# A decode layer: K and V in 4 MB transfers, weights ahead of K, and the output halves in two column tiles

## The chip, the cores and the metric

The kernel runs on one core of a Trainium2 chip. The metric is the device time of one launch in microseconds (us). The time before the change is 224.56 us, the median of three runs (223.5, 224.56, 224.62).

## What is computed

One decode step for four sequences (B = 4), one new position each, width D = 576. Two branches start from the same x and are added to it.

```python
def _A_ref(x, k_cache, v_cache, wq, wo):        # attention; 32 query heads, 16 K/V heads, Dh = 128
    W = 2048                                    # only the last 2048 of 8192 cached positions
    q = (x @ wq).reshape(B, 1, 32, 128)
    k, v = k_cache[:, :, Sk - W:], v_cache[:, :, Sk - W:]     # each serves two query heads
    p = softmax(q k^T * Dh ** -0.5)
    return (p v).reshape(B, 1, 4096) @ wo
def _B_ref(x, w1, w2, w3, w4):
    h = gelu(layernorm(x) @ w1)
    hs = shifted(h) @ w2                        # four groups of columns moved by 1 or 2 positions
    x1 = x + hs
    return x1 + gelu(layernorm(x1) @ w3) @ w4
xn = layernorm(x)
return x + _A_ref(xn, k_cache, v_cache, wq, wo) + _B_ref(xn, w1, w2, w3, w4)
```

With a single position the shifts move everything out, so `hs` is zero; the kernel multiplies w2 by a tile of zeros (`hs_inT`). All data are bfloat16. 88.5 MB come in: K and V 33.5 MB each, w3 and w4 5.3 MB each, wq and wo 4.7 MB each, w1 and w2 0.7 MB each. The output is 4 x 576.

## The kernel before, in words

**Order of work.** There is no scheduler. Every piece of work is entered by `add` (or `add_dma` for transfers) with an engine, the events that it waits for, the event that it signals, and a key; each engine's list is then sorted by key and written out. All large transfers are issued by SyncE (SP), in one queue, in the order of their keys (L171). Before it issues a transfer, SP waits for the events in its list, and everything behind it in the list waits too.

**Memory.** K and V pass through a ring of ten slots of 2 MB. A slot is 128 partitions of 16 KB: four heads of one sequence, 32 partitions to a head, 64 consecutive positions to a partition (`NU = 4`, `NT = 64`), so 16 chunks of K and 16 of V. Weights borrow slots that are free for a time: wq stands in slots 8 and 9 at the start, wo in slots 4 to 7 after K, w3 and w4 in slots that V has left.

**K stage.** A chunk's 64 blocks of 128 x 128 are transposed by TensorE against a permutation matrix, eight to a PSUM buffer (`pe_T`, L333; three buffers, `NTB`). VectorE and ScalarE copy them out (`evac`, L340 and L339). `pe_SC` (L351) multiplies them by the queries: four matmuls with 512 columns each, one for each head, go to the four 32-column tiles of the array. All 16 chunks add into four PSUM banks, with zeros in the padded queries `Qpad` for the rows of other heads.

**Softmax.** One reduction over the four banks gives the row maximum (L372), ScalarE takes the exponential bank by bank (L376), VectorE multiplies each bank by the head masks (L384, 16 instructions), and two rounds of matmuls (L393, L404), with copies by ScalarE (L402, L406), turn the probabilities so that positions lie on partitions.

**V stage.** For each chunk VectorE spreads the probabilities over the heads (`dve_pad`, L422), and `pe_PV` (L433) does 64 matmuls with V blocks as weights. V0 to V7 wait until K chunks 6 to 13 are transposed; V8 to V15 wait for PV0 to PV7. Between V7 and V8 the queue has w1, w2 and wo, which wait for the last probability turn (`PTy3`).

**MLP and end.** The small products (w1 at L493/L495, w2 at L503/L504), a layernorm (`ln_ops`) and x1's transpose (L283/L286) are placed among PV8 to PV12. wo is applied in three parts (`pe_AO`, L456) after PV7, PV11 and PV15; each needs a scaled copy (L472), selecting matmuls (L449) and a copy (L475). The product with w3 (`pe_h2`, L525 and L529, 180 matmuls) stands after the last wo part, then one gelu (L535), then w4 in five pieces of 18, 10, 5, 2 and 1 rows to a partition, each with its own transfer and its matmuls (also L456). wo and w4 add into the same two PSUM accumulators, one for each half of the 576 output columns: for each row of weights there is a 288-column matmul for the left half, then one for the right half, both with a 128 x 4 weight in the same array columns. VectorE and ScalarE copy one half each to SBUF (L550, L551), and SP and ScalarE store them.

The lines that the prediction's steps touch are L171 (all transfers), L333, L351, L372, L376, L384, L393, L422, L433, L456, L525/L529 and L550/L551.

Of the kernel before, what the change touches and what calls it, by code (L numbers as in the profile page):

```python
# [5 lines left out]
FP32 = mybir.dt.float32  # L6
# [6 lines left out]
NSLOT = 10  # L13
NKT = 12
NTB = 3
SC_LAG = 2
ACT_EVAC = (1, 4, 7)
N_WARM = 6
AO_CH = ((0, 4), (4, 6), (6, 8))
# [14 lines left out]
def bass_parallel_sum__sliding_block_cached__mixer_s_mlp__decode_kernel(  # L34
# [8 lines left out]
    NU = 4  # L43
# [11 lines left out]
    CH = [(b, gq) for gq in range(4) for b in range(B)]  # L55
# [3 lines left out]
    with ExitStack() as ctx:  # L59
# [5 lines left out]

        ring_t = sb("ring", [128, NSLOT * UE], BF16)
        regB_t = sb("regB", [128, NKT * 1024], BF16)
        PT_t = sb("PT", [128, NT * 32], BF16)
# [3 lines left out]
        ktgrp = regB_t[:].rearrange("p (s t u i) -> p s t u i", s=NKT // 2, t=16, u=NU)  # L72
        P4 = regB_t[:, 0:4 * NU * 512].rearrange("p (q t u i) -> p q t u i", q=4, t=16, u=NU)
        PTx = regB_t[:, 4 * NU * 512:4 * NU * 512 + 4 * 512].rearrange("p (q x) -> p q x", q=4)
        PTpad = regB_t[:, 0:2 * NT * 2 * NU].rearrange("p (s t u e) -> p s t u e", s=2, t=NT, u=NU)
        PTv = PT_t[:].rearrange("p (t c e) -> p t c e", t=NT, c=NC)

        wqmain = ring_t[:, 8 * UE:10 * UE].rearrange("p (r n) -> p r n", r=4)
        wqrag = PT_t[:, 0:Hq * Dh // 2]
        wo_a = ring_t[:, 4 * UE:4 * UE + 7 * 4 * D].rearrange("p (h r n) -> p h r n", h=7, r=4)  # L80
        _o = 2 * NT * 2 * NU
        wo_b = regB_t[:, _o:_o + 4 * D].rearrange("p (r n) -> p r n", r=4)
        _o += 4 * D
        w1main = regB_t[:, _o:_o + 4 * D].rearrange("p (r n) -> p r n", r=4)
        _o += 4 * D
        w1rag = regB_t[:, _o:_o + HALF]
        _o += HALF
        w2main = regB_t[:, _o:_o + 4 * D].rearrange("p (r n) -> p r n", r=4)
        _o += 4 * D
        w2rag = regB_t[:, _o:_o + HALF]  # L90
        _o += HALF
        assert _o <= NKT * 1024
        wo_at = lambda hg: wo_a[:, hg] if hg < 7 else wo_b
        w3r = [ring_t[:, 6 * UE + r * F:6 * UE + (r + 1) * F] for r in range(3)] + [ring_t[:, 8 * UE:8 * UE + F]]
        w3rag = ring_t[:, 6 * UE + 3 * F:6 * UE + 3 * F + FH]
        assert 3 * F + FH <= 2 * UE
# [23 lines left out]
        mask4 = sb("mask4", [128, NU], FP32)  # L120
        sel_f = sb("sel_f", [128, 32], FP32)
        sel_bf = sb("sel_bf", [128, 32], BF16)
# [3 lines left out]
        zeros_bf = sb("zeros_bf", [128, 512], BF16)  # L126
        rmax = sb("rmax", [128, 1], FP32)
# [7 lines left out]
        ORT = sb("ORT", [128, 4, 8, B], BF16)  # L135
        t1 = sb("t1", [B, D], FP32)
        out_sb = x1n_bf
# [4 lines left out]
        PTps = [ps[:, 4 + k, :].rearrange("p (t x) -> p t x", t=16) for k in range(4)]  # L142
        ACC = [ps[0:B, k, 0:HALF] for k in range(2)]
        ORps = ps[:, 2, 0:128].rearrange("p (r h b) -> p r h b", r=4, h=8)
        rinvps = ps[:, 3, 0:128]
        OTps = [ps[:, 6 - max(gq - 1, 0), 0:128] for gq in range(4)]
        QTps = ps[:, 7, 0:128]
        HSps = ps[0:B, 7, 128:128 + HALF]
        HTps = ps[:, 7, 416:440].rearrange("p (c b) -> p c b", b=B)
        XTps = [ps[:, 7, 440 + 12 * k:452 + 12 * k].bitcast(BF16).rearrange("p (c b) -> p c b", b=B) for k in range(3)]  # L150
        H2Tps = ps[:, 7, 0:144].rearrange("p (c b) -> p c b", b=B)
# [25 lines left out]

        KS = float(NB + 4)
# [6 lines left out]
        def pool_ident(t, tag, pattern, view, key):  # L185
# [11 lines left out]
        P(lambda e: e.memset(ones_f[:], 1.0), sig="ones_f", key=-89)  # L197


        add("dve", lambda e: e.tensor_reduce(out=mask4[:], in_=ident_f[:].rearrange("p (u x) -> p u x", u=NU), axis=AX.X, op=ALU.add),  # L200
            waits=["ident_f"], sig="mask4", key=-8)
        add("dve", lambda e: e.tensor_reduce(out=sel_f[:], in_=ident_f[:].rearrange("p (u x) -> p x u", u=NU), axis=AX.X, op=ALU.add),
            waits=["ident_f"], sig="sel_f", key=-8)
        add("dve", lambda e: e.tensor_copy(out=sel_bf[:], in_=sel_f[:]), waits=["sel_f"], sig="sel_bf", key=-7.9)
        add("dve", lambda e: e.tensor_reduce(out=mU[:], in_=ident_f[:].rearrange("p (i u) -> p u i", u=NU), axis=AX.X, op=ALU.add),
            waits=["ident_f"], sig="mU", key=-8)
        for x in range(2):
            add("dve", lambda e, x=x: e.tensor_copy(out=mU_bf[:, :, x], in_=mU[:]), waits=["mU"], sig=f"mU_bf{x}", key=-7.8)
# [3 lines left out]
        ev_wq = [add_dma([(ring_t[:, 8 * UE:10 * UE], A_wq[0:512, :].rearrange("(p r) n -> p (r n)", r=4))], "wq", (), -20),  # L212
                 add_dma([(wqrag, rag_src(A_wq))], "wqr", (), -15)]

        def kv_src(cache, c):
            b, gq = CH[c]
            return cache[b, NU * gq:NU * gq + NU, Sk - W:Sk, :].rearrange("g (i t) d -> i g (t d)", t=NT)

        k_slot = lambda c: c % NSLOT
        v_slot = lambda c: (6, 7, 8, 9, 0, 1, 2, 3)[c % 8]  # L220
        t_done = lambda c: f"T{NBLK * c + NBLK - 1}"
        ev_k, ev_v = [], []
        for c in range(NC):
            w = ["q"] if c in (8, 9) else ([t_done(c - NSLOT)] if c >= NSLOT else [])
            ev_k.append(add_dma([(slot(k_slot(c)), kv_src(A_k_cache, c))], ("ring", k_slot(c)), w, c))
        for c in range(NC):
            w = [f"PV{c - 8}"] if c >= 8 else [t_done(c + 6)]
            ev_v.append(add_dma([(slot(v_slot(c)), kv_src(A_v_cache, c))], ("ring", v_slot(c)), w, KS + c))
            if c == 7:
                free = ["PTy3"]  # L230
                ev_w1 = add_dma([(w1main, B_w1[0:512, :].rearrange("(p r) n -> p r n", r=4)), (w1rag, rag_src(B_w1))], "w1",
                                free, KS + c + 0.1)
                ev_w2 = add_dma([(w2main, B_w2[0:512, :].rearrange("(p r) n -> p r n", r=4)), (w2rag, rag_src(B_w2))], "w2",
                                free, KS + c + 0.2)
                wo_s = A_wo.rearrange("(h p r) n -> p h (r n)", h=8, r=4)
                ev_wo = add_dma([(wo_a.rearrange("p h r n -> p h (r n)"), wo_s[:, 0:7, :]),
                                 (wo_b.rearrange("p r n -> p (r n)"), wo_s[:, 7, :])],
                                "wo", [t_done(NC - 1)] + free, KS + c + 0.3)
        w3_src = B_w3[0:512, :].rearrange("(p r) n -> p r n", r=4)
        ev_w3 = [add_dma([(w3r[r], w3_src[:, r, :])], ("w3", r), ["PV10" if r == 3 else "PV9"], KT + r) for r in range(4)]  # L240
        ev_w3.append(add_dma([(w3rag, rag_src(B_w3))], ("w3", 4), ["PV9"], KT + 4))
        w4tile, w4cols, ev_w4, W4N = [], [], [], []
        base = 0
        offs = (8 * UE + F, 0, 10 * D, 15 * D, 17 * D)
        assert F + 18 * D <= 2 * UE and 18 * D <= 2 * UE
        for n, rc in enumerate(W4_ROWS):
            v = ring_t[:, offs[n]:offs[n] + rc * D]
            ev_w4.append(add_dma([(v, B_w4[base:base + 128 * rc, :].rearrange("(p r) n -> p (r n)", r=rc))], ("w4", n),
                                 ["PV11" if n == 0 else "PV13"], KT + 5 + n))
            W4N.append((len(w4tile), len(w4tile) + rc))  # L250
            for r in range(rc):
                w4tile.append(v[:, r * D:(r + 1) * D])
                w4cols.append((base + r, base + 128 * rc, rc))
            base += 128 * rc
        assert len(w4tile) == 36 and base == F
        ev_o = [None, None]
        for h, eng in ((0, "sp"), (1, "act")):
            ev_o[h] = add_dma([(o2[:, HALF * h:HALF * (h + 1)], out_sb[:, HALF * h:HALF * (h + 1)])], ("out", h),
# [34 lines left out]
        add("dve", lambda e: e.tensor_copy(out=xnT[:], in_=XTps[0]), waits=["xT"], sig="xnT", key=-39)  # L293

# [20 lines left out]
        add("pe", pe_xT(xn2_bf, 1), waits=["ln2", "qT"], sig="x2T", key=-20)  # L315
        add("dve", lambda e: e.tensor_copy(out=xn2T[:], in_=XTps[1]), waits=["x2T"], sig="xn2T", key=-9)

        def pe_warm(e):
            ins = None
            for w in range(N_WARM):  # L320
                ins = e.matmul(ps[:, 4 + (w % NTB), :], lhsT=zeros_bf[:, 0:128], rhs=zeros_bf[:, :], start=True, stop=True)  # L321
            return ins
# [3 lines left out]

        def pe_T(n):
            c, k = n // NBLK, n % NBLK

            def f(e):  # L330
                ins = None
                for t in range(8):
                    ins = e.transpose(tb[n % NTB][:, t, :], slot_t(k_slot(c))[:, 8 * k + t, :], perm_bf[:])  # L333
                return ins
            return f

        def evac(n):
# [294 lines left out]
```

## Time and profile before

| | us |
|---|---|
| median of the runs (lowest, highest) | 224.56 (223.5, 224.62) |
| span of the profiled execution, first to last instruction | 222.3 |
| time around the span (median less span; the page has no time of its own for the profiled execution) | 2.3 |
| first transposes to last scores | 21.0 to 103.5 |
| last scores to first V matmul | 103.5 to 114.4 |
| V matmuls | 114.4 to 192.1 |
| w3 product | 196.7 to 206.7 |
| w4 product | 209.0 to 220.1 |

The page is read as follows. Part 1 gives busy time per engine, part 2 the same in 40 slices of 5.6 us, with the granted TensorE clock, the share of time that the 16 transfer engines were busy, and the rate. Part 3 lists the queues. Part 4 follows the chain of work that ended last backwards. Part 5 groups instructions by line, part 6 the transfers, with the median time from issue to landing. Besides the page, the trace answers for a stretch of time: busy time per engine, clock and rate, or the instructions in order. It also holds a record of each packet that a transfer engine moved and of each landing; a transfer's packets are the contiguous runs that go to one partition, eight partitions to each of the 16 engines.

### The profile page before, as it was taken

What the parts mean: (1) busy time and instruction counts of PE and PEld (TensorE: products, weight loads), DVE (VectorE), ACT (ScalarE), POOL (GpSimd) and SP (SyncE); (2) the same over time, 40 slices, a digit from 0 to 9 for tenths busy, and PEclk for the clock granted to TensorE, in tenths of its full rate; (3) what the DMA queues carried; (4) which work ended last, traced back from release to release, by engine and by line L of the source; (5) the groups of instructions that cost most, each with busy time, mean ns of one, the idle gap of its engine ahead of it and who ended that gap; (6) DMA issues with size and microseconds to landing.
All of it is one profiled execution on the core that took longest, in us unless ns stands there. A gap on an engine that the chain in (4) does not pass through costs nothing.

```text
span 222.3 us, 6311 instructions
## 1 busy us (share of the span) xinstructions
PE 162.3 (73%) x2964; PEld 126.4 (57%) x2966; DVE 76.9 (35%) x162; ACT 61.2 (28%) x75; POOL 5.5 (2%) x17
## 2 busy tenths in 40 slices
PE   0068999999999999995377653001948996699596
PEld 0065777777777777773257653001545584489363
DVE  4303656666666655666822111000150010000000
ACT  2000655556556665555860000000002000000000
POOL 8100000000000000000000000000000000000000
PEclk9999999999999999999655555555555697585589
DMA  7999999999999999999999999999999999999820
GB/s 284 407 410 425 436 431 419 420 428 431 428 431 422 422 431 428 423 422 422 425 428 425 433 405 401 413 438 428 428 425 419 428 431 415 421 426 428 359 109 1
DMA packets 8017, 88.90 MB, mean 400 GB/s; under 512 B 812, under 2 KB 1208, under 8 KB 3000
## 3 DMA queue, kind: packets, MB, share of 16 engines
q1 hardware_dynamic: 7976, 88.50, 94.7%
q8 instruction: 23, 0.38, 0.7%
q14 instruction: 2, 0.02, 0.0%
q10 hardware_dynamic: 16, 0.01, 0.0%
HBM read 88.49 MB, written 0.00 MB: 398 GB/s over the span
## 4 chain that ended last, share of the span: by engine, by line
DMA 56%; PE 41%; ACT 1%; issue 1%; SPq 1%; DVE 0%
DMA ring<-in_A_v_cache_dram 34%; PE ps L333 25%; DMA ring<-in_B_w_dram 16%; PE ps L351 6%; DMA ring<-in_A_wq_dram 6%; PE ps L456 5%; PE ps L304 2%; PE ps L433 2%; PE ps L321 1%; ACT regB L339 1%; SPq L171 1%; DVE Qpad L313 0%; ACT x1n_bf L551 0%; PE ps L283 0%; PE ps L286 0%
## 5 line engine op out<-in xcount | busy, mean ns | idle before, releaser
L333 PE MATMUL ps<-perm_bf,ring 128*128 128x128 bf16 x1024 | 66.7, 221 | 0.5 <-ACT regB L339 0.4
L333 PEld LDWEIGHTS ps<-perm_bf,ring 128*128 128x128 bf16 x1024 | 58.0, 98 | 13.5 <-issue 6.9
L340 DVE COPY regB<-ps 128x1024 bf16<-128x1024 bf16 x80 | 52.3, 687 | 29.9 <-PE ps L333 28.1
L339 ACT ACTIVATE regB<-ps 128x1024 bf16<-128x1024 bf16 x48 | 47.5, 1022 | 48.8 <-PE ps L333 48.8
L433 PE MATMUL ps<-regB,ring 128*128 128x8 bf16 x1024 | 29.0, 168 | 33.8 <-DMA ring<-in_A_v_cache_dram 27.8
L433 PEld LDWEIGHTS ps<-regB,ring 128*128 128x128 bf16 x1024 | 28.3, 103 | 37.1 <-issue 31.8
L351 PE MATMUL ps<-regB,Qpad 128*32 128x512 bf16 x256 | 16.9, 382 | 0.4 <-ACT regB L339 0.4
L269 ACT ACTIVATE sd<-mv 4x1 f32<-4x1 f32 x3 | 0.6, 202 | 51.1 <-DVE mv L267 51.1
L456 PE MATMUL ps<-ring,h2T_sb 128*4 128x288 bf16 x72 | 11.1, 325 | 2.3 <-DMA ring<-in_B_w_dram 2.3
L422 DVE TENSOR_TENSOR regB<-PT,mU_bf 128x512 bf16<-128x512 bf16 x16 | 6.6, 419 | 15.9 <-PE ps L433 13.8
L456 PE MATMUL ps<-ring,ORT 128*4 128x288 bf16 x56 | 11.3, 380 | 0.3 <-DVE ORT L475 0.3
L535 ACT ACTIVATE h2T_sb<-ps 128x144 bf16<-128x144 f32 x1 | 0.3, 292 | 37.3 <-PE ps L529 37.3
L456 PEld LDWEIGHTS ps<-ring,h2T_sb 128*4 128x4 bf16 x72 | 6.8, 95 | 6.3 <-DMA ring<-in_B_w_dram 2.4
L475 DVE CAST ORT<-ps 128x32 bf16<-128x32 f32 (+1 forms) x3 | 0.6, 203 | 26.7 <-PE ps L449 26.7
L550 DVE CAST x1n_bf<-ps 4x288 bf16<-4x288 f32 x1 | 0.4, 446 | 27.0 <-PE ps L456 27.0
L304 PE MATMUL ps<-xnT,ring 128*128 128x4 bf16 x128 | 3.6, 166 | 7.9 <-DMA ring<-in_A_wq_dram 7.9
L351 PEld LDWEIGHTS ps<-regB,Qpad 128*32 128x32 bf16 x256 | 5.3, 95 | 6.0 <-issue 0.9
L456 PEld LDWEIGHTS ps<-ring,ORT 128*4 128x4 bf16 x56 | 5.8, 107 | 4.5 <-DVE ORT L475 0.4
L525 PEld LDWEIGHTS ps<-x1nT,ring 128*128 128x128 bf16 x144 | 8.0, 152 | 0.2 <-issue 0.2
L525 PE MATMUL ps<-x1nT,ring 128*128 128x4 bf16 x144 | 8.1, 194 | 0.0
L304 PEld LDWEIGHTS ps<-xnT,ring 128*128 128x128 bf16 x128 | 3.5, 104 | 7.9 <-DMA ring<-in_A_wq_dram 7.9
L472 DVE TENSOR_TENSOR OTn<-ps,rinvB 128x32 bf16<-128x32 f32 (+1 forms) x3 | 0.6, 202 | 18.5 <-PE ps L433 18.5
(92 smaller groups left out, 72.3 us busy)
## 6 DMA issues: line engine op xcount, KB each, us to landing
ring<-in_A_k_cache_dram SPq DMA_DIRECT2D x16, 2048.0 KB, 43.3
ring<-in_A_v_cache_dram SPq DMA_DIRECT2D x16, 2048.0 KB, 43.1
ring<-in_B_w_dram SPq DMA_DIRECT2D x4, 1152.0 KB, 33.4
ring<-in_A_wq_dram SPq DMA_DIRECT2D x1, 4096.0 KB, 12.3
ring<-in_A_wo_dram SPq DMA_DIRECT2D x1, 4032.0 KB, 32.1
ring<-in_B_w_dram SPq DMA_DIRECT2D x1, 2592.0 KB, 36.6
ring<-in_B_w_dram SPq DMA_DIRECT2D x1, 1440.0 KB, 30.3
regB<-in_B_w_dram SPq DMA_DIRECT2D x2, 576.0 KB, 21.3
```

Of the source, the lines that this page charges most:

```text
L171: e.dma_start(o_, i_).then_inc(S[skey], 16)
L269: add("act", lambda e: e.activation(out=sd[:, idx:idx + 1], in_=mv[:, idx, 1:2], func=ACTF.Sqrt, bias=EPS, scale=1.0), waits=[f"{tag}_mv"] ...
L304: ins = e.matmul(QTps[:, B * h:B * (h + 1)], lhsT=w, rhs=x_, start=(r == 0 and h == 0), stop=(r == 4), skip_group_check=True)
L321: ins = e.matmul(ps[:, 4 + (w % NTB), :], lhsT=zeros_bf[:, 0:128], rhs=zeros_bf[:, :], start=True, stop=True)
L333: ins = e.transpose(tb[n % NTB][:, t, :], slot_t(k_slot(c))[:, 8 * k + t, :], perm_bf[:])
L339: return "act", lambda e: e.activation(out=ktbuf[:, n % NKT], in_=tb[n % NTB], func=ACTF.Copy)
L340: return "dve", lambda e: e.tensor_copy(out=ktbuf[:, n % NKT], in_=tb[n % NTB])
L351: ins = e.matmul(Sps[32 * u:32 * u + 32, q, :].rearrange("p (t i) -> p t i", t=16), lhsT=Qpad_t[:, qo:qo + 32], rhs=ktgrp[:, s % (NKT // 2 ...
L422: return lambda e: e.tensor_tensor(out=PTpad[:, c % 2], in0=PTv[:, :, cc, :].unsqueeze(2).to_broadcast([128, NT, NU, 2]), in1=mU_bf[:].uns ...
L433: ins = e.matmul(o_, lhsT=slot_t(v_slot(c))[:, t, :], rhs=PTpad[:, c % 2, t].rearrange("p u e -> p (u e)"), start=(t == 0), stop=(t == NT ...
L456: return e.matmul(ACC[h], lhsT=lhsT, rhs=rhs, start=start, stop=stop)
L525: ins = e.matmul(H2Tps[:, n, :], lhsT=w3r[r][:, lo:hi:st], rhs=x1nT[:, r, :], start=(r == 0 and n == 0), stop=False, skip_group_check=True)
```

## The change

- K and V come in chunks of eight heads: 16 partitions to a head, 128 positions to a partition, 32 KB to a partition, 4 MB to a transfer (`NU = 8`). The ring has four such slots, 16 MB. There are 8 chunks of K and 8 of V; the last V chunk comes in two halves.
- Everything that depends on the head count of a chunk follows: eight score matmuls to a group, eight masks to a bank (32 mask instructions), 128 probability matmuls with 16 columns, pads of 2048 elements, 128 V matmuls with 16 columns to a chunk. The row maximum is taken bank by bank. The transposes have four PSUM buffers in place of three, eight transposed blocks in SBUF in place of twelve.
- SP issues wq, w1, w2 and w3 ahead of K; w3 has a region of its own (`regX`), which wo takes over in two halves. The small products, x1 and the whole w3 product with its gelu stand before the first transpose.
- V0 to V2 wait until K4 to K6 are transposed; V3 waits for the last probability matmul (`PTp3`), because the masked probabilities lie in its slot; V4 to V7 wait for PV0 to PV3. wo's halves are issued after V2 and after V5. w4 waits for PV4 and PV5.
- wo is applied in two halves, each with 16 rows to a partition (18 KB runs). The reshuffle before it is a transpose, a masked copy, eight accumulating matmuls with a selection matrix `Z`, and a copy.
- The two output halves accumulate in two 32-column tiles of the array (partitions 0 to 3 and 32 to 35 of two banks), and the output tile has 36 rows.
- The engines' lists are written without an `nc.Block`.

```diff
-NSLOT = 10
-NKT = 12
-NTB = 3
-SC_LAG = 2
+NSLOT = 4
+NKT = 8
+NTB = 4
+SC_LAG = 3
...
-    NU = 4
+    NU = 8
...
-    CH = [(b, gq) for gq in range(4) for b in range(B)]
+    CH = [(b, gh) for gh in range(2) for b in range(B)]
...
+        regX_t = sb("regX", [128, 4 * F + FH], BF16)
...
+        P8 = slot(3).rearrange("p (q t u i) -> p q t u i", q=4, t=32, u=NU)
...
-        ACC = [ps[0:B, k, 0:HALF] for k in range(2)]
+        ACC = [ps[0:B, 0, 0:HALF], ps[32:32 + B, 1, 0:HALF]]
...
+        ev_w1 = add_dma([(w1main.rearrange("p r n -> p (r n)"), main_src(B_w1)), (w1rag, rag_src(B_w1))], "w1", (), -14)
+        ev_w2 = add_dma([(w2main.rearrange("p r n -> p (r n)"), main_src(B_w2)), (w2rag, rag_src(B_w2))], "w2", (), -13)
+        ev_w3 = add_dma([(w3main, main_src(B_w3)), (w3rag, rag_src(B_w3))], "w3", (), -12)
...
         for c in range(NC):
-            w = ["q"] if c in (8, 9) else ([t_done(c - NSLOT)] if c >= NSLOT else [])
-            ev_k.append(add_dma([(slot(k_slot(c)), kv_src(A_k_cache, c))], ("ring", k_slot(c)), w, c))
+            w = {2: ["q"], 3: ["q", "hT", "x1"]}.get(c, [])
+            if c >= NSLOT:
+                w = [t_done(c - NSLOT)]
+            ev_k.append(add_dma([(slot(c % NSLOT), kv_src(A_k_cache, c))], ("ring", c % NSLOT), w, c))
+
+        def wo_dma(g, key):
+            src = A_wo[2048 * g:2048 * (g + 1), :].rearrange("(p r) n -> p (r n)", r=16)
+            ev_wo.append(add_dma([(wo_h[g], src)], ("wo", g), ["h2_4"], key))
         for c in range(NC):
-            w = [f"PV{c - 8}"] if c >= 8 else [t_done(c + 6)]
-            ev_v.append(add_dma([(slot(v_slot(c)), kv_src(A_v_cache, c))], ("ring", v_slot(c)), w, KS + c))
...
+            w = [f"PV{c - 4}"] if c >= 4 else ([t_done(c + 4)] if c < 3 else ["PTp3"])
+            if c == 3:
+                wo_dma(0, KS + c - 0.1)
+            if c == 6:
+                wo_dma(1, KS + c - 0.1)
...
-                                 ["PV11" if n == 0 else "PV13"], KT + 5 + n))
+                                 ["PV4" if n == 0 else "PV5"], KT + 5 + n))
...
-        for r in range(5):
-            add("pe", pe_h2(r), waits=[ev_w3[r]] + (["x1nT", "gelu_h"] if r == 0 else []), sig=f"h2_{r}", key=KT + r)
+        for r in range(5):
+            add("pe", pe_h2(r), waits=[ev_w3] + (["x1nT"] if r == 0 else []), sig=f"h2_{r}", key=-17 + r)
...
-        add("dve", lambda e: e.tensor_reduce(out=rmax[:], in_=Sps, axis=AX.XY, op=ALU.max), waits=[f"SC{NS - 1}"], sig="rmax", key=KS)
+        for q in range(4):
+            add("dve", lambda e, q=q: e.tensor_reduce(out=rmax4[:, q:q + 1], in_=Sps[:, q, :], axis=AX.X, op=ALU.max),
...
-                    ins = e.tensor_scalar(out=P4[:, q, :, u, :], in0=P_sb[:, q, :].rearrange("p (t i) -> p t i", t=16),
-                                          scalar1=mask4[:, u:u + 1], scalar2=None, op0=ALU.mult)
+                    ins = e.tensor_scalar(out=P8[:, q, :, u, :], in0=P_sb[:, q, :].rearrange("p (t i) -> p t i", t=32),
+                                          scalar1=mask8[:, u:u + 1], scalar2=None, op0=ALU.mult)
...
-        def acc_mm(e, h, lhsT, rhs, start=False, stop=False):
-            return e.matmul(ACC[h], lhsT=lhsT, rhs=rhs, start=start, stop=stop)
+        def acc_mm(e, h, lhsT, rhs, stop=False):
+            return e.matmul(ACC[h], lhsT=lhsT, rhs=rhs, start=False, stop=stop, tile_position=(0, 32 * h), skip_group_check=True)
...
+        def pe_sel(g):
+            def f(e):
+                ins = None
+                for dq in range(8):
+                    ins = e.matmul(ORps[g].rearrange("p b r -> p (b r)"), lhsT=Z[:, g, 7 - dq:135 - dq],
+                                   rhs=OTm[:, dq].rearrange("p b r -> p (b r)"), start=(dq == 0), stop=(dq == 7))
+                return ins
+            return f
...
+                for r in range(16):
+                    for h in range(2):
+                        ins = acc_mm(e, h, ORT[:, g, r, :], wo_h[g][:, r * D + HALF * h:r * D + HALF * (h + 1)])
...
-        with nc.Block() as block:
...
+        for nm, engine in (("sp", nc.sync), ("pool", nc.gpsimd), ("dve", nc.vector), ("act", nc.scalar), ("pe", nc.tensor)):
+            emit_program(nm, engine)
```

## The prediction

> **What bounds the kernel now.** I read the page from the top: the busy shares, then the slices, then the chain that ended last, and after that the stretches around the end of the run and the timeline of the tail.
>
> ```profile
> span 222.3 us, 6311 instructions
> PE 162.3 (73%) x2964; PEld 126.4 (57%) x2966; DVE 76.9 (35%) x162; ACT 61.2 (28%) x75; POOL 5.5 (2%) x17
> PEclk9999999999999999999655555555555697585589
> DMA  7999999999999999999999999999999999999820
> GB/s 284 407 410 425 436 431 419 420 428 431 428 431 422 422 431 428 423 422 422 425 428 425 433 405 401 413 438 428 428 425 419 428 431 415 421 426 428 359 109 1
> q1 hardware_dynamic: 7976, 88.50, 94.7%
> DMA 56%; PE 41%; ACT 1%; issue 1%; SPq 1%; DVE 0%
> ```
>
> No compute engine is busy all the time; the transfers are, from the second slice to the 37th, at some 425 GB/s. 88.5 MB have to come in, and the queue never runs dry, so the floor of this kernel is the end of its last transfer plus what must follow it. The next three show that last part.
>
> ```profile
> 192.00:203.00 11.00, 10.42 (x155) 8.48 (x152) 0.38 (x2) 0.00 (x0) 0.00 (x0) 0.66 1.03 429
> 203.00:209.00 6.00, 3.72 (x70) 3.64 (x69) 0.00 (x0) 0.29 (x1) 0.00 (x0) 0.50 0.96 405
> 209.00:213.30 4.30, 4.30 (x19) 2.27 (x20) 0.00 (x0) 0.00 (x0) 0.00 (x0) 0.50 0.59 238
> 213.30:220.10 6.80, 6.78 (x55) 4.51 (x53) 0.11 (x1) 0.00 (x0) 0.00 (x0) 1.00 0.08 31
> ```
> ```profile
> 196.68 8.06 PE L525 MATMUL ps<-x1nT,ring 128*128 128x4 bf16 x144
> 204.60 2.12 PE L529 MATMUL ps<-x1nT,ring 128*128 128x4 bf16 x36
> 208.99 11.09 PE L456 MATMUL ps<-ring,h2T_sb 128*4 128x288 bf16 x72 [2.28 <-DMA ring<-in_B_w_dram]
> 219.99 0.45 DVE L550 CAST x1n_bf<-ps 4x288 bf16<-4x288 f32 x1 [26.96 <-PE ps L456]
> 220.12 0.40 ACT L551 ACTIVATE x1n_bf<-ps 4x288 bf16<-4x288 f32 x1 [13.07 <-PE ps L456]
> ```
> ```profile
> ring<-in_B_w_dram SPq DMA_DIRECT2D x1, 2592.0 KB, 36.6
> ring<-in_B_w_dram SPq DMA_DIRECT2D x1, 144.0 KB, 31.8
> ```
>
> (Columns of the first: stretch, its length, busy time of PE, weight loads, DVE, ACT, POOL, granted clock, DMA share, GB/s.) The last piece of w4 was issued at 183.4 and landed 31.8 later, at 215.2. The first, 2.6 MB, landed at 208.95, and only then did the 72 output matmuls start. They took 11.1 us: about 240 ns each at clock 0.5 until 213.3 (18 in 4.3 us), about 125 ns at 1.0. So TensorE ended 4.9 us behind the last byte, and 2.17 us (220.09 to 222.26) went to evacuation, store and stop. A smaller span has two sources only: an earlier last byte, or less than 4.9 us behind it.
>
> **The change part by part.** All the bytes stay, so I follow the transfer queue first.
>
> *Longer runs.* The trace's transfer records give the time of a packet: 611 ns for 16 KB (median 613), 1213 to 1240 for 32 KB (the steady part of wq), 182 for 4.6 KB, 351 for 9.2 KB, 774 for 20.7 KB. Each of 16 engines carries 8 partitions. K and the first seven V chunks: 15 transfers x 8 packets x (2 x 611 - 1213 = 9 ns) = 1.1 us saved. w3 (9.2 KB becoming 36.9 KB): 32 x 351 = 11.2 against 8 x 1365 (at 32 KB's rate) = 10.9, saves 0.3. wo (4.6 becoming 18.4 KB): 64 x 182 = 11.6 against 16 x 690 = 11.0, saves 0.6. Together 2.0 us, and the last byte lands at 213.2. Bounds: at 1240 ns the K and V gain turns into 15 x 8 x 18 = 2.2 us of loss (last byte 216.5); the low bound is 1213. I take 1213, because wq's last 48 packets all lie at 1213 to 1224 and the slower ones fall beside start-up.
>
> *Does the queue stay full?* The ring shrinks from 20 to 16 MB, and 11.3 MB of weights now stand ahead of K. On the rows of before, wqr lands at 14.3; w1 and w2 add 3.4, w3 12.4 (30.1), each K chunk 9.7 (39.8 to 107.8), V0 to V2 29.1 (136.9), the first wo half 5.5 (142.4). TensorE: wq's matmuls end at 17.6 as now, the w3 product cannot start before 30.1 and takes 10.2 (both rows above), the six warm-up matmuls 2.6 cold, so the K stage starts near 42.9, 22 us later than now (21.0). It took 82.5 us for the same 1024 transposes and 256 score matmuls, so it ends near 125.4 (118 if the fourth PSUM buffer lets it follow the transfers). Every K slot is freed in time: K4's at 53, needed at 69; V0's, V1's, V2's at 93, 104, 114, needed at 108, 117, 127.
>
> The tight one is V3, whose slot holds the masked probabilities. It now waits for all four probability transposes, and the other V chunks, wo's second half and w4 are queued behind it on SP. After the scores: maximum and bias 1.2 (the 2.29 us reduction is split in four, one left behind the scores), first exp 0.7, masks 32 instead of 16 at 0.268 (4.29 us for 16) = 8.6, last 32 transposes 1.2 (0.61 for 16): 137.4. The packets ahead run out at 140.8 (142.4 less the 1.6 us between last packet and landing), and issue to first packet was 1.0. Margin 2.4 us; cost zero while it holds. V4 to V7 wait for PV0 to PV3: pad 1.6 (4 x 0.41), 128 matmuls 3.6, giving issues at 144, 148, 152 and 157 against needs from 151 on. The two w4 waits (PV4, PV5) clear near 167 and 177, needed at 196. The queue stays full.
>
> *Moved off the end.* The w3 product (10.2 us on TensorE, between the last attention product and w4) and the small MLP go to the front, where TensorE waited 7.9 us for wq and now waits for w3. This costs the K stage its 22 us, which the queue covers as just shown. In exchange nothing but V7's second half, its reshuffle and wo's second half stands before w4.
>
> *The tail.* V7's second half lands 12.4 us of w4 before the end, at 200.8. 64 matmuls 1.85 (202.6); scale 0.2, transpose, masked copy 0.6 (a quarter of 2.29 for 512 elements out of PSUM), 8 selecting matmuls 0.5, copy 0.2 with hand-overs: 204.6. Then 16 pairs of wo and 36 pairs of w4. The price of a pair has no row; the nearest is the score product, where four 512-column matmuls in four column tiles start within 10 ns of each other, every 215 ns.
>
> ```profile
> 27.00 0.98 PE ps L351 x16
> ```
>
> Sixteen in 0.98 us is not sixteen times 213. So a pair costs between one matmul (120 ns warm, 240 cold) and two (240, 480); I take one, the nearer row. The clock rose 4.3 us into steady work (208.99 to 213.3), so about 208.9 here. wo: 16 pairs cold 3.8 (208.5); w4's first piece landed 207.0, 2 pairs cold, 16 warm: 210.9; second piece (landed 210.4) 212.1; third (212.1) 212.8; fourth 213.1; the last (213.2) 213.4. If the clock rises 2.5 us later, 214.3. Middle 213.8, or 0.6 us behind the last byte against 4.9.
>
> *Small things.* New memsets on POOL and mask reductions on DVE (seven of some 0.35 us) lie under the wait for w3, before 42.9; if that cover were gone they would cost 3 us once. The PV pads grow from 6.6 to 13 us, under the V transfers. SP issues fewer instructions (half as many for K and V, 0.54 us each). The branches of the engine blocks go; bound 0 to 0.5 us, taken 0.
>
> *Sum.* 222.3 - 2.0 (last byte) - 4.3 (behind it) = 216.0 span. The median of the runs, 224.56, lies 2.3 above the profiled span; the runs lie 1.1 apart. 216.0 + 2.3 = **218.3 us**.
>
> [...] Heads lie 2 MB apart in the caches; now four are read at once at 128 KB steps, the change reads eight at 256 KB steps. At four, the K transfers of 2 MB landed 4.89 us apart, 429 GB/s, the full rate of this trace. [...]
>
> **The rivals.**
>
> *Eight heads at once lower the transfer rate* (slower). For: more of the streams then stand at the same offset of a 2 MB pitch than in any row of this trace. Against: no loss at four, and one engine's pace is 26.3 to 27.0 GB/s for every packet length from 9 KB up, as if the engine itself set it. It decides from the point where K and V lose 6.3 us of 155, that is 32 KB packets of 1265 ns in place of 1213. With the mean of wq's packets, start-up included (1307), 15 x 8 x 94 ns = 11.3 us: 229.6.
>
> *The clock stays at 0.5 to the end.* For: it was 0.5 from 107.5 to 175.8 under gappy work. 52 pairs x 240 from 204.6 = 217.1; +2.2 + 2.3 = 221.6.
>
> *The two column tiles do not overlap* (that the change does not do what it says). For: only four tiles were seen overlapping, with 32-column weights. 104 matmuls from 204.6: 18 cold to 208.9, 86 x 122 ns = 10.5: 219.4; 223.9.
>
> *The queue runs dry at V3.* The masks write runs of 16 elements instead of 32; at double price they add 8.6 us, V3's first packet comes at 147 and the bubble is 6.2 us: 224.5. Against: the same element type and count. It decides above a 2.4 us delay.
>
> **How the numbers follow.** Main case 0.68 (218.3; its own range 216 to 220.5 from the clock's phase and the packet bounds), cold tail 0.11 (221.6), no overlap 0.06 (223.9), dry queue 0.05 (224.5), slower transfers 0.10 (226 to 235). Faster by over 0.5% (below 223.4; 0.5% is about what a measurement of this kernel can tell from none): main and cold, 0.79. Same: no overlap and dry queue, 0.11. Slower: 0.10. The range runs to 224.0, past the cold tail and the two-matmul bound of a pair, and down to 215.3, where the slowest transfer engine, now 3 us behind the median one, catches up by a third.
>
> **What would show it.** Right: DMA share at 9 tenths from the second slice until some 10 us before the end; K landings 9.7 us apart; the last w4 piece at about 213; the w3 product at 30 to 40 us, transposes from 43; V3's issue near 137 with no dent in the rate behind it; the output matmuls in pairs that start together and TensorE's end within 1.5 us of the last landing. Wrong: landings more than 10.1 us apart, a dent near 140 us, or 100 matmuls that start one by one.

## The result, and the profile after

The changed kernel takes **380.06 us** (median of 4 runs, 379.28 to 392.66) against 224.18 us before (4 runs, 223.5 to 224.62) on the same chip: 1.69 times as long (1.6935, 95% interval 1.6882 to 1.6989). The forecast was 218.3 us, its range 215.3 to 224.0, and "slower" had 0.10. The execution of 392.66 was in a slower state that some executions show, and the ratio leaves it out. The profiled execution took 379.28 us, with a span of 377.8.

The page of the changed kernel, its busy shares, slices of 9.4 us, and the queue:

```profile
span 377.8 us, 6354 instructions
PE 167.4 (44%) x2997; PEld 132.8 (35%) x3000; DVE 87.9 (23%) x181; ACT 60.9 (16%) x74; POOL 5.8 (2%) x20
...
PEclk9999999777867768595969655555555555655558
DMA  8999999999999999999999999999999999999993
GB/s 334 430 395 250 219 217 201 210 217 208 217 220 212 210 219 217 212 210 223 210 220 213 215 220 217 205 293 209 212 215 224 219 203 277 211 219 243 246 391 131
...
q1 hardware_dynamic: 4616, 88.49, 97.7%
```

The same 88.49 MB come in as before, and the transfer engines are as busy as before, 9 tenths in every slice but the ends. But from the fourth slice, where the weights end and K begins, they move some 215 GB/s in place of 425. It rises in slices 27 and 34 (293 and 277), about where wo passes, and at the end (391), where w4 does. So the busy share, the same at both rates, shows here only that packets are under way, and not how fast they go.

The groups of the same page, and stretches of the changed kernel (columns as before: stretch, length, PE, weight loads, DVE, ACT, POOL, granted clock, DMA share, GB/s):

```profile
L405 PE MATMUL ps<-perm_bf,ring 128*128 128x128 bf16 x1024 | 78.0, 244 | 61.1 <-DMA ring<-in_A_k_cache_dram 61.1
L510 PE MATMUL ps<-regB,ring 128*128 128x16 bf16 x1024 | 28.9, 174 | 109.8 <-DMA ring<-in_A_v_cache_dram 106.5
...
ring<-in_A_k_cache_dram SPq DMA_DIRECT2D x8, 4096.0 KB, 68.1
```
```profile
55.00:204.00 149.00, 94.31 (x1263) 73.63 (x1260) 54.53 (x82) 47.25 (x47) 0.00 (x0) 0.78 1.00 214
204.00:220.00 16.00, 6.36 (x150) 4.50 (x148) 11.00 (x40) 9.54 (x18) 0.00 (x0) 0.69 0.98 214
220.00:345.00 125.00, 28.51 (x815) 24.01 (x815) 10.77 (x12) 0.00 (x0) 0.00 (x0) 0.51 1.00 225
```

TensorE now waits for K (61.1 us) and for V (106.5 us). The landings in the trace give the pace: K0 to K7 from 54.5 to 193.3 us, 19.8 apart, where the prediction had 9.7. The packet records show where that comes from: a 32 KB packet of K or V takes 2488 ns (median of 1920), one of wq, which is just as long, 1217 (median of 128) in the same execution.

And the end of the changed kernel, in its timeline:

```profile
367.67 3.43 PE L524 MATMUL ps<-regX,ORT 128*4 128x288 bf16 x32 [0.39 <-DVE ORT L562]
370.93 4.94 PE L524 MATMUL ps<-ring,h2T_sb 128*4 128x288 bf16 x72
...
375.90 0.45 DVE L580 CAST out_sb<-ps 4x288 bf16<-4x288 f32 x1 [8.29 <-PE ps L524]
```

The last byte landed at 375.54, and TensorE ended some 0.3 us later (4.9 before). What the change was to do at the end, it did. So two questions stand: what halves the transfers, and whether the rest of the forecast holds without that.

### The profile page after: what moved, and what is told of

It reads as the page before. It is cut to its first block, busy times and chain, and to the rows that moved or that the text cites. A ratio compares the mean times of both kernels' runs of the same rounds, so it can differ in the third digit from the quotient of the medians.

```text
span 377.8 us, 6354 instructions
## 1 busy us (share of the span) xinstructions
PE 167.4 (44%) x2997; PEld 132.8 (35%) x3000; DVE 87.9 (23%) x181; ACT 60.9 (16%) x74; POOL 5.8 (2%) x20
## 3 DMA queue, kind: packets, MB, share of 16 engines
q1 hardware_dynamic: 4616, 88.49, 97.7%
HBM read 88.49 MB, written 0.00 MB: 234 GB/s over the span
## 4 chain that ended last, share of the span: by engine, by line
another core or an unknown queue 42%; PE 38%; DMA 13%; DVE 3%; SPq 1%; issue 1%; ACT 1%; DVEq 0%
PE ps L405 20%; DMA ring<-in_A_k_cache_dram 13%; PE ps L510 8%; PE ps L423 5%; PE ps L524 3%; DVE ring L461 2%; SPq L176 1%; DVE regB L499 0%; PE ps L528 0%; PE ps L535 0%; PE ps L527 0%; ACT regB L411 0%; PE ps L470 0%; ACT Qpad L453 0%
## 5 line engine op out<-in xcount | busy, mean ns | idle before, releaser
L405 PE MATMUL ps<-perm_bf,ring 128*128 128x128 bf16 x1024 | 78.0, 244 | 61.1 <-DMA ring<-in_A_k_cache_dram 61.1
L405 PEld LDWEIGHTS ps<-perm_bf,ring 128*128 128x128 bf16 x1024 | 70.7, 111 | 78.8 <-DMA ring<-in_A_k_cache_dram 63.2
L510 PE MATMUL ps<-regB,ring 128*128 128x16 bf16 x1024 | 28.9, 174 | 109.8 <-DMA ring<-in_A_v_cache_dram 106.5
L423 PE MATMUL ps<-regB,Qpad 128*32 128x512 bf16 x256 | 22.2, 429 | 1.2 <-ACT regB L411 1.2
L499 DVE TENSOR_TENSOR regB<-regB,mU_bf 128x2048 bf16<-128x2048 bf16 x8 | 9.7, 1220 | 27.6 <-PE ps L510 25.0
L386 PE MATMUL ps<-x1nT,regX 128*128 128x4 bf16 x144 | 8.2, 195 | 11.1 <-DMA regX<-in_B_w_dram 11.1
L386 PEld LDWEIGHTS ps<-x1nT,regX 128*128 128x128 bf16 x144 | 8.1, 155 | 11.2 <-DMA regX<-in_B_w_dram 11.2
L461 DVE TENSOR_SCALAR ring<-Qpad,mask 128x512 bf16<-128x512 bf16 x32 | 8.5, 346 | 0.8 <-ACT Qpad L453 0.8
L524 PE MATMUL ps<-regX,ORT 128*4 128x288 bf16 x64 | 7.0, 404 | 0.8 <-DVE ORT L562 0.8
L524 PE MATMUL ps<-ring,h2T_sb 128*4 128x288 bf16 x72 | 4.9, 286 | 0.0
```

Source lines behind the costliest of these rows:

```text
L386: ins = e.matmul(H2Tps[:, n, :], lhsT=w3r[r][:, lo:hi:st], rhs=x1nT[:, r, :], start=(r == 0 and n == 0), stop=False, skip_group_check=True)
L405: ins = e.transpose(tb[n % NTB][:, t, :], slot_t(c % NSLOT)[:, 8 * k + t, :], perm_bf[:])
L423: ins = e.matmul(Sps[32 * uu:32 * uu + 32, q, :].rearrange("p (t i) -> p t i", t=32), lhsT=Qpad_t[:, qo:qo + 32], rhs=ktgrp[:, s % 2, :, u ...
L461: ins = e.tensor_scalar(out=P8[:, q, :, u, :], in0=P_sb[:, q, :].rearrange("p (t i) -> p t i", t=32), scalar1=mask8[:, u:u + 1], scalar2=N ...
L499: return lambda e: e.tensor_tensor(out=PTpad[:, c % 2], in0=PTv[:, :, cc, :].unsqueeze(2).to_broadcast([128, NT, NU, 2]), in1=mU_bf[:].uns ...
L510: ins = e.matmul(o_, lhsT=slot_t(c % NSLOT)[:, t, :], rhs=PTpad[:, c % 2, t].rearrange("p u e -> p (u e)"), start=(t == 0), stop=(t == NT ...
```

## The experiments

### Which transfer patterns are slow

A kernel that only reads, in twelve stretches of drained transfers from K's cache. In each, the source is a grid of runs and heads, whose slower dimension (the outer count) comes first. The lines shown are stretches 1 to 3, 5, 6 and 9: count of runs, count of heads, length of a run, its pitch, the heads' pitch, transfers. Each of the reading kernels was executed once; a rate in their tables is a stretch's bytes over the time from the start of its first packet to the end of its last.

```diff
+    ("ig", 32, 4, 16 * KB, 16 * KB, 2 * MB, 4),
+    ("ig", 16, 8, 32 * KB, 32 * KB, 2 * MB, 3),
+    ("ig", 16, 8, 32 * KB, 32 * KB, 512 * KB, 3),
...
+    ("ig", 32, 4, 32 * KB, 32 * KB, 2 * MB, 3),
+    ("ig", 16, 8, 16 * KB, 16 * KB, 2 * MB, 4),
...
+    ("lin", 0, 0, 32 * KB, 0, 0, 3),
```

> Transfers alone, no arithmetic: the kernel reads pieces of the K cache in twelve patterns, one after the other, each with the queue drained before it, and writes x back as output (all of attention and MLP left out). Each pattern has 128 runs to a transfer, written as sets of (runs per head, heads, run length, pitch from run to run, pitch from head to head). Pattern 1 is the layout of before (32, 4, 16 KB, 16 KB, 2 MB), pattern 2 that of the changed kernel (16, 8, 32 KB, 32 KB, 2 MB). Theory A, eight streams at a 2 MB pitch fall on the same memory channels: pattern 1 near 611 ns a packet, pattern 2 near 2478 ns, pattern 3 (pitch 512 KB in place of 2 MB) and pattern 4 (2 MB + 32 KB) back at 1213 ns, pattern 6 (8 heads, 16 KB runs at 16 KB pitch) slow at over 1000 ns, pattern 5 (4 heads, 32 KB runs) fast. Theory B, long runs at a 32 KB pitch do it, whatever the heads: patterns 2, 3, 4, 5 and 8 slow near 2478 ns, pattern 6 fast near 611. Theory C, the way eight inner runs fall on engines and partitions does it, whatever the addresses: patterns 2, 3, 4, 6, 7 and 12 all at twice the time, 1, 5, 8 and 9 fast. Pattern 7 is 8 heads with 16 KB out of every 32 KB, 8 is two heads, 9 one contiguous stretch, 10 has 16 heads with one head to an engine, 11 is pattern 1 with a 512 KB pitch, 12 is pattern 2 with every second run skipped.

| stretch | outer x inner | run | head pitch | GB/s | ns of a packet (median) |
|---|---|---|---|---|---|
| 1 | 32 x 4 | 16 KB | 2 MB | 414 | 611 |
| 2 | 16 x 8 | 32 KB | 2 MB | 209 | 2551 |
| 3 | 16 x 8 | 32 KB | 512 KB | 211 | 2529 |
| 4 | 16 x 8 | 32 KB | 2 MB + 32 KB | 209 | 2548 |
| 5 | 32 x 4 | 32 KB | 2 MB | 417 | 1213 |
| 6 | 16 x 8 | 16 KB | 2 MB | 211 | 1262 |
| 7 | 16 x 8 | 16 KB of every 32 | 2 MB | 215 | 1251 |
| 8 | 64 x 2 | 32 KB | 2 MB | 417 | 1213 |
| 9 | contiguous | 32 KB | | 416 | 1213 |
| 10 | 16 heads x 8 runs | 32 KB | 2 MB | 206 | 2553 |
| 11 | 32 x 4 | 16 KB | 512 KB | 410 | 611 |
| 12 | 16 x 8 | 32 KB of every 64 | 2 MB | 208 | 2547 |

What is slow is the outer count of 16 with eight inside, with both run lengths, every pitch tried, and with runs or heads outermost. This is what theory C expected, in all the patterns that it names; A wanted 3 and 4 fast, and B wanted 5 and 8 slow. 4 MB transfers (5, 9) and 32 KB runs (5, 8, 9) are at full rate. That takes the addresses out: no pitch made a difference here (414 at 2 MB and 410 at 512 KB, both with 32 outside; 209, 211 and 209 with 16).

### The changed kernel with four heads

If the layout of K and V is the whole loss, then the changed kernel with its other parts kept must meet the forecast.

```diff
-NSLOT = 4
+NSLOT = 8
...
-    NU = 8
+    NU = 4
...
-    CH = [(b, gh) for gh in range(2) for b in range(B)]
+    CH = [(b, gq) for gq in range(4) for b in range(B)]
...
-            w = {2: ["q"], 3: ["q", "hT", "x1"]}.get(c, [])
+            w = {4: ["q"], 5: ["q"], 6: ["q", "hT", "x1"]}.get(c, [])
...
-            w = [f"PV{c - 4}"] if c >= 4 else ([t_done(c + 4)] if c < 3 else ["PTp3"])
-            if c == 3:
+            w = [f"PV{c - 8}"] if c >= 8 else ([t_done(c + 8)] if c < 7 else ["PTp3"])
+            if c == 7:
```

(and, following from these, the slots of the weights, the masks, and w4's waits for PV9 and PV11, wo's second half behind V11; the last V chunk, of 2 MB, is no longer halved.)

> The changed kernel with one thing undone: chunks of four heads, 32 runs of 16 KB to a head, 2 MB to a transfer, eight slots (the same 16 MB of ring); weights and w3 ahead of K, wo in two halves with 18 KB runs, the w3 product at the front and the output halves in two column tiles all stay. Theory 1 (the source pattern with an outer count of 16 is the whole loss, the rest of the prediction stands): K landings 4.9 us apart, last piece of w4 near 213, TensorE's end within 1.5 us of it, 216 to 221 us in all, near 218.8 (the predicted 218.3 without the 1.1 us for 32 KB runs, plus what 2 MB chunks let in earlier). Theory 2 (weights ahead of K or the smaller ring also cost): still full packets of 611 ns, but a dent in the rate between K and V or behind V7, and more than 224 us. Theory 3 (the pattern is not the cause in the full kernel): over 300 us.

Measured: **218.18 us** (4 runs, 218.08 to 218.62) against 223.79, ratio 0.9747 (0.9702 to 0.9792). It beats both kernels. Its K chunks land 4.9 us apart. Its page, stretches and timeline:

```profile
span 216.9 us, 6246 instructions
...
DMA  8999999999999999999999999999999999999972
GB/s 285 393 393 476 435 388 429 414 432 422 423 429 426 432 429 420 426 420 423 425 432 429 423 423 423 429 425 430 423 429 417 428 429 421 432 429 431 418 326 77
```
```profile
37.00:120.00 83.00, 82.76 (x1326) 65.49 (x1327) 51.74 (x77) 45.73 (x47) 0.00 (x0) 1.00 1.01 426
120.00:138.00 18.00, 11.21 (x242) 8.18 (x240) 10.97 (x32) 10.38 (x19) 0.00 (x0) 0.72 1.00 424
138.00:200.00 62.00, 29.81 (x884) 25.59 (x884) 6.39 (x16) 0.00 (x0) 0.00 (x0) 0.53 1.01 427
200.00:209.00 9.00, 5.10 (x93) 3.68 (x95) 1.22 (x3) 0.00 (x0) 0.00 (x0) 0.50 0.97 409
209.00:215.00 6.00, 6.00 (x88) 3.53 (x82) 0.00 (x0) 0.00 (x0) 0.00 (x0) 0.92 0.42 169
```
```profile
206.70 3.69 PE L511 MATMUL ps<-regX,ORT 128*4 128x288 bf16 x32 [0.39 <-DVE ORT L549]
...
210.23 4.78 PE L511 MATMUL ps<-ring,h2T_sb 128*4 128x288 bf16 x72
```

The DMA share is the same as in the changed kernel, and the rate is twice as high. The difference of the spans, 160.9 us (377.8 - 216.9), lies in the landings thus: w3's last piece lands 3.6 us later (35.3 against 31.6; its short packets are queued beside K0); from there to the last of V it takes 328.1 us against 170.6, of which the two halves of wo, mixed with V's packets, take 21.2 against 11.0. So K and V themselves cost 147.3 us, wo 10.2, w3 3.6, and w4 -0.2. All of it goes with the eight heads.

### Source or destination

Again a kernel that only reads; the lines shown are stretches 1 to 7 of ten (destination, first partition, runs, heads, pieces, length, two pitches, transfers).

```diff
+    ("sb", 0, 32, 4, 1, 16 * KB, 16 * KB, 2 * MB, 4),
+    ("sb", 0, 16, 8, 1, 16 * KB, 16 * KB, 2 * MB, 4),
+    ("hbm", 0, 32, 4, 1, 16 * KB, 16 * KB, 2 * MB, 4),
+    ("hbm", 0, 16, 8, 1, 16 * KB, 16 * KB, 2 * MB, 4),
+    ("sb", 0, 16, 4, 1, 32 * KB, 32 * KB, 2 * MB, 4),
+    ("sb", 0, 32, 2, 1, 32 * KB, 32 * KB, 2 * MB, 4),
+    ("sb", 64, 16, 4, 1, 32 * KB, 32 * KB, 2 * MB, 4),
```

> Transfers alone again (attention and MLP left out, x is written back). Ten patterns, each drained before the next; all runs from the K cache with 2 MB between heads. 1: outer 32, four heads, 16 KB, into 128 SBUF partitions. 2: outer 16, eight heads, 16 KB, the same. 3 and 4: the same two with a target in main memory in place of SBUF. 5: outer 16, four heads, 32 KB, into partitions 0 to 63; 6: outer 32, two heads, 32 KB, into 0 to 63; 7: as 5 into 64 to 127. 8: outer 64, two heads, 16 KB, 128 partitions. 9 and 10: outer 16 with eight heads and outer 32 with four heads at 4 KB runs. [...] Theory S (the source side or the engines themselves are halved by an outer count of 16): 4 at half the rate of 3, 6 faster than 5. [...]

Into SBUF the two patterns gave 412 and 217 GB/s (611 and 1242 ns for 16 KB); into main memory the same reads gave 324 and 314 (734 and 760 ns). So the reading is not what is slow. And 64 partitions gave half the rate with either outer count: 206, 205 and 209 GB/s in stretches 5 to 7. Theory S, by which 4 has half the rate of 3 and 6 is faster than 5, is out. Of the last three, 64 x 2 gave 406, and runs of 4 KB 223 (16 x 8) and 296 (32 x 4), or 276 against 159 ns a packet, 1.7 times as long, where 16 KB took 2.0 times as long. So the loss is there at every length tried and is smaller at 4 KB, and it shows with SBUF as the target and not with main memory.

### Which partitions

A 16 x 8 transfer has 16 landings, one of 8 outer rows 8, one of 4 rows 4: I take it that an engine gets the partitions of one outer row, so eight neighbours in a 16 x 8 transfer. Every transfer into 64 partitions so far began at partition 0 or 64 and was slow (205 to 209 GB/s). The test is to move the same transfer by 32 partitions, and by 16 (first partition, outer, inner, transfers; runs of 32 KB); that such a move could matter was a guess.

```diff
+PHASES = (
+    (0, 8, 8, 4),
+    (32, 8, 8, 4),
+    (0, 4, 8, 4),
+    (16, 8, 8, 4),
+    (0, 16, 4, 4),
+    (32, 16, 4, 4),
+)
```

> Left out: the whole layer; only K is read, in six stretches of four transfers each with 32 KB runs, eight or four heads, into chosen partitions, each stretch drained before the next; the output is x. An engine gets the partitions of one outer row. [...] Theory N (an outer count of 16 or 8 is slow whatever the partitions, or the engine itself is slow where its partitions are eight neighbours): stretches 1, 2 and 4 alike, near 2550, and 3 too; 5 and 6 alike. Theory H (64 partitions give half the rate wherever they lie): 5 and 6 both near 205 GB/s, 1 and 2 alike.

| stretch | partitions | engines | GB/s | ns of a packet (median) | packets under 1400 / 1400 to 2000 / over 2000 |
|---|---|---|---|---|---|
| 1 | 0-63 | 8 | 107 | 2504 | 0 / 2 / 254 |
| 2 | 32-95 | 8 | 212 | 1213 | 252 / 4 / 0 |
| 3 | 0-31 | 4 | 105 | 1213 | 124 / 2 / 2 |
| 4 | 16-79 | 8 | 108 | 2270 | 0 / 43 / 213 |
| 5 | 0-63 | 16 | 205 | 2554 | 0 / 3 / 253 |
| 6 | 32-95 | 16 | 413 | 1213 | 239 / 17 / 0 |

The slices of this kernel's page (7.8 us each; stretch 5 is the 33rd to 36th, stretch 6 the 38th to 40th):

```profile
DMA  4444555445255453222223554544442699996896
GB/s 102 101 101 101 109 118 109 101 105 122 76 219 219 202 236 143 93 109 109 109 109 84 118 118 101 122 114 122 122 122 50 139 202 202 202 202 135 345 463 270
```

The same transfer, read in the same way, from the same addresses and into 64 partitions, has 205 GB/s on 0-63 and 413 on 32-95. So it is the destination partitions that decide between these two, and neither the outer count, nor eight neighbours to an engine (stretches 2 and 3 have them, at 1213 ns), nor the number of partitions (64 in both). That rules out theory N, which had stretches 1 and 2 alike (2504 and 1213 ns), and theory H, which had 5 and 6 both near 205 GB/s. What makes 0-63 slow was not shown, nor why 32 x 4 and 16 x 8, which fill the same 128 partitions, run at 414 and 209 GB/s; the runs show only that the outer count matters there.

Stretch 4, on 16-79, is slow too (108 GB/s, against 212 on 32-95): none of its packets were under 1400 ns. By the landings four engines finished the four transfers 1.8, 3.3, 5.5 and 8.4 us ahead of the other four (means), which is 2.06 us a packet against 2.33 (from the first landing to the fourth, 24 packets). So half of its engines ran a little ahead of the others, and none at the 1213 ns of 32-95.

### Engines out of step

Before the last test my guess was that engines hold each other up because they go through their eight partitions in step; then some that start a few packets late should run free. So this kernel, which ran before the one above, sets some engines back. The second, fourth and fifth stretch begin with a small transfer that holds up four engines by four packets, eight engines by four, and four by two.

```diff
+FULL = (16, 8, 3)
+PHASES = (
+    (FULL,),
+    ((4, 4, 1), FULL),
+    (FULL,),
+    ((8, 4, 1), FULL),
+    ((4, 2, 1), FULL),
+)
```

> Transfers alone (attention and MLP left out, x is written back), five stretches, each drained before the next; every stretch has three transfers with outer 16, eight heads, 32 KB runs into 128 partitions. 1 and 3: nothing ahead of them. 2: one transfer with outer 4 and four heads (16 partitions, so four packets on each of at most four engines) queued ahead. 4: outer 8 and four heads (eight engines, four packets each) ahead. 5: outer 4 and two heads (two packets on each of four engines) ahead. [...]

No stretch got faster: 209, 201, 210, 199 and 196 GB/s, with medians of 2551, 2533, 2522, 2513 and 2542 ns, though the four engines that were held up landed 6.4 to 6.8 us behind the last of the others, some 2.6 packets, in the first two transfers of the second stretch. Had the guess held, many of that stretch's packets would have come near the 1213 ns of the fast stretches; 8 of 400 were under 1400. So with the lags tried here the halving does not hang on engines going through the partitions in step. What slows a packet, here and in stretch 4 above, stays open.

### The column tiles

Two runs split the gain of the four-head version: that version with both output halves in one column tile, and the kernel before with the column tiles alone.

```diff
-        ACC = [ps[0:B, 0, 0:HALF], ps[32:32 + B, 1, 0:HALF]]
+        ACC = [ps[0:B, k, 0:HALF] for k in range(2)]
...
-            return e.matmul(ACC[h], lhsT=lhsT, rhs=rhs, start=False, stop=stop, tile_position=(0, 32 * h), skip_group_check=True)
+            return e.matmul(ACC[h], lhsT=lhsT, rhs=rhs, start=False, stop=stop, skip_group_check=True)
```

> The four-head kernel (e1_four_heads) with the column tiles undone: both output halves accumulate in the same array columns, as before. If the tiles carry the tail: wo and w4 are 104 matmuls from 206.7, 240 ns each until the clock rises some 4 us later and 122 ns after that, so TensorE ends near 221 instead of 215.0, and the time is 223.5 to 225.5, at par with the kernel before, whatever else was moved. If moving the w3 product and wo to the front is what carries it: under 220.5.

Measured: 224.87 us (10 runs) against 224.25, ratio 1.0027 (1.0004 to 1.0051): no gain left, as the first of the two cases had it. Its tail:

```profile
206.72 6.55 PE L511 MATMUL ps<-regX,ORT 128*4 128x288 bf16 x32 [0.39 <-DVE ORT L549]
213.11 8.98 PE L511 MATMUL ps<-ring,h2T_sb 128*4 128x288 bf16 x72
```

```diff
-        ACC = [ps[0:B, k, 0:HALF] for k in range(2)]
+        ACC = [ps[0:B, 0, 0:HALF], ps[32:32 + B, 1, 0:HALF]]
...
-            return e.matmul(ACC[h], lhsT=lhsT, rhs=rhs, start=start, stop=stop)
+            return e.matmul(ACC[h], lhsT=lhsT, rhs=rhs, start=False, stop=stop, tile_position=(0, 32 * h), skip_group_check=True)
```

> The kernel before with the column tiles alone added (a 36-row start for the accumulators and its own output tile come with them). If the tiles carry the tail: the w4 product starts at 209.0 as before and takes 6.4 us instead of 11.1 (36 pairs, 18 at 240 ns, 18 at 122), the end moves from 220.1 to 215.6, still ahead of nothing later than the last landing at 215.2, and the time is 219 to 220.5. If a pair costs two matmuls: 223 to 225.

Measured: 219.82 us (4 runs, 219.61 to 220.0), ratio 0.9797 (0.9756 to 0.9838). Its tail:

```profile
209.03 6.93 PE L459 MATMUL ps<-ring,h2T_sb 128*4 128x288 bf16 x72 [3.47 <-DMA ring<-in_B_w_dram]
```

These matmuls start in pairs: in the four-head trace the two of a pair are at most 0.01 us apart, and pairs follow each other every 0.24 us until the clock rises at 209.9 and every 0.12 us behind that. In the one-tile version single matmuls follow each other at these same distances, and its 72 take 8.98 us at a granted clock of 1.00, against 4.78 at 1.00 in pairs.

The column tiles alone are worth 2.0% (1.6 to 2.4), about 4.4 us; with the weights moved ahead and the longer runs of wo and w3 it is 2.5% (2.1 to 3.0). The intervals overlap, so the other moves are worth about 1 us with the tiles, if that. Without the tiles they are worth nothing, because the wo part then ends 6.4 us after the start at 206.7, past the landing of w4's first two pieces, and w4's 72 matmuls are serial.

## Why the prediction was wrong

- *Longer runs* is the step that failed. It gave the 32 KB packets of K and V 1213 ns, bounded by 1240 from wq's packets. In the kernel they took 2488, and the step's 1.1 us of saving was a loss of 147 us against the four-head version, with 14 us more in w3 and wo, which pass beside K and V. The row was of the right length and of the wrong split over the partitions: wq's 128 rows are contiguous, and a contiguous source ran at 1213 in stretch 9 too. A packet's time was taken as a property of its length ("as if the engine itself set it"). Into SBUF it was, in these runs, also one of the destination (1213 on 32-95, 2554 on 0-63 for the same transfer) and of the split (1213 at 32 x 4 and 2551 at 16 x 8 into 128 partitions), and in the trace of before all lengths from 9 KB up went at one pace (26.3 to 27.0 GB/s to an engine), so no bound taken from there could show this.
- *The rival "Eight heads at once lower the transfer rate"* named the sign and the place, with 0.10, and its point of decision (1265 ns) was passed by far. Its price, 229.6 us in a range of 226 to 235, was wrong by 150 us, for the same reason: the mean of wq's packets is no bound for another pattern. Its mechanism, more streams at one offset of a 2 MB pitch, fell with stretches 3 and 4 of the first experiment (211 and 209 GB/s at two other pitches, 209 at this one).
- *Does the queue stay full?* Yes. With four heads the rate is 426, 424 and 427 GB/s through the three stages, the K stage ended at 124.2 us (125.4 forecast), and the chunk that waits for the last probability matmul was issued at 131.2 (137.4 forecast for its counterpart V3, behind 16 masks more, or 4.3 us), with no dent behind it. The eight-head form of that wait was not tried at the full rate. Two numbers of that step are off: the parts listed behind the scores (1.2, 0.7, 8.6 and 1.2) end at 137.1, not 137.4, and in the trace of before the last packets of wq, wqr and w4's pieces ended 0.3 to 0.5 us ahead of their landings, where the sum took 1.6. Both make the stated margin of 2.4 us too small. In the changed kernel itself the queue was full too, only slow, so "DMA share at 9 tenths" came true and proved nothing; the landings 9.7 us apart were the sign that told, and they failed.
- *Moved off the end* was right. In the four-head version transposes ran from 44 us on (42.9 forecast) and TensorE was busy in 82.76 of the 83 us from 37 to 120, under the transfers.
- *The tail* was right in its mechanism and near in size: TensorE ended 0.3 us behind the last byte (0.6 forecast) in both the changed kernel and the four-head one. Sixteen wo pairs took 3.69 us (3.8 forecast), 231 ns a pair; in one tile 32 matmuls took 6.55. The clock rose at 209.9 in the four-head version and at 370.4 in the changed kernel, just ahead of w4's product. So the rivals of a cold tail and of tiles that don't overlap are both out; the second one's price (223.9) was near what the kernel without tiles measured (224.87).
- *The last byte* was to come 2.0 us earlier. In the four-head version, which keeps 16 KB runs for K and V and so had 0.9 to gain by the step's terms, it landed 0.5 earlier (214.7 against 215.2).
- *The sum* of 218.3 us agrees with the four-head version (218.18). That is partly luck: its span is 216.9 and not 216.0, since the last byte came 1.5 us later than forecast, and the time around the span is 1.4 us (218.25 - 216.9) where the sum took 2.3. Executions of the kernel before that list both have 1.7 to 1.8, so the 2.3, a median less another execution's span, was too long. And the low end of the range does not follow as stated: a third of 3 us takes 218.3 to 217.3; 215.3 needs the whole 3 us. But for the packets of K and V, the terms that the four-head version tests were right to within about 1.5 us.

## What to carry to other kernels

When a transfer's shape changes, look at which partitions it fills and at what outer count, and compare these, not only the packet length, with a row at the known rate; transfers of 16 or 32 outer rows into 64 partitions ran at 205 to 209 GB/s on 0-63 and 64-127 here, and at 413 on 32-95. For a two-level source into 128 partitions an outer count of 32 or 64 kept 406 to 417 GB/s, one of 16 gave 206 to 217 (runs of 16 and 32 KB). A busy share near 1.0 did not show that the queue was at its rate (1.00 at 214 GB/s, 1.01 at 426): read bytes per time beside it, and packet times beside the lengths.

## What the hardware showed that was not expected

- The same 2 MB transfer, 16 engines with four partitions each, runs at 205 GB/s into partitions 0-63 and at 413 into 32-95.
- The halving held also when some engines start several packets late (196 to 201 GB/s), and transfers into 16-79 had none of their 256 packets under 1400 ns (median 2270).
- 72 matmuls of 288 columns in two column tiles took 4.78 us, the last of them waiting for landings, and in one tile 8.98, both at a granted clock of 1.00.
- From main memory to main memory both patterns ran at 314 to 324 GB/s, below the 412 of the good pattern into SBUF and above the 217 of the bad one.
